# A gated mix of two attentions: two token blocks' sum moves and the value weights held behind the key-value products, and sixteen double steps with new orders of work

## The chip, the cores and the metric

The kernel runs on one core of a Trainium2 chip. The time is the device time of one execution in microseconds (us). Three executions of the kernel before took 321.81, 322.15 and 322.46 us, with a median of 322.15. One more execution was recorded by the hardware profiler; it took 322.69 us, of which the recorded span is 321.0.

The core has five engines with instruction streams of their own, which meet only at semaphores: TensorE (PE in the profile; its weight loads are shown as PEld), VectorE (DVE), ScalarE (ACT), GpSimd (POOL) and SyncE (SP), which here issues nearly all DMA transfers.

## The reference

The input x has 2048 tokens of 640 features; there are 32 heads of 20 features. Two attentions are computed from the same x and mixed by a gate per token:

```
g   = sigmoid(sum(x * gate_w))
out = g * A(x) + (1 - g) * B(x)

A: q, k, v = x @ wqkv;  pq, pk = q @ w_phi, k @ w_phi  (per head)
   phi(t) = [softmax(t), softmax(-t)]
   kv = phi(pk)^T v (head by head);  z = sum over tokens of phi(pk)
   A  = ((phi(pq) @ kv) / (phi(pq) . z + 1e-6)) @ wo

B: four segments of 512 tokens, one after the other; per head
   a_dot = causal softmax attention within the segment
   a_mem = (phi(q) @ M) / (phi(q) . z)        phi(t) = t + 1 if t > 0 else exp(t)
   o     = sigmoid(beta) * a_mem + (1 - sigmoid(beta)) * a_dot
   M, z grow by phi(k)^T v and sum of phi(k) after each segment
   B     = o @ wo
```

## The kernel before, in words

The order of instructions on every engine is written out by hand: each engine runs its instructions in the order in which the program emits them, and waits at the head of its queue until the semaphores of that instruction are there. There is no planner but the small one of the double steps (below).

**Key stage (from 10 to 56 us).** For each of 16 blocks of 128 tokens (`emit_a1`, L235 to L247) TensorE makes keys and values, ScalarE the exponentials, VectorE the sums and reciprocals, and GpSimd (VectorE for block 15) multiplies the normalised key features into `EkSn`. Right behind each block `emit_zmove` (L255) issues two transfers on SP, one for each sign. They copy 16 x 8 x 640 numbers of `EkSn` into rows of the tile `Z`, so that the sum z over all tokens can be made by adding 32 column groups of `Z` on VectorE. Block 14 fills groups 16 to 23 of part of the rows, block 15 groups 24 to 31.

**Key-value products (56 to 65 us).** `emit_kv` (L373) multiplies `EkSn` with the values, 312 small matmuls, in five accumulators `kv_ps`; `emit_kvn` (L387, VectorE) masks each into `kvn`. Between them `emit_zadd` (L263) adds column groups of `Z`: groups 1 to 8 before the last accumulator is masked, and 9 to 31 after the gate. The gate is `emit_gate` (L346, L349 on TensorE, L351 on ScalarE) and `emit_gS` (L354 to L356, three small VectorE instructions). VectorE has them in front of the remaining 46 additions.

**Weights of B.** `WvB`, `WkB`, `WqB` and the two output weights are loaded on SP after this (L437, L442). A copy of two columns on GpSimd (L435), which reads the fourth `kvn`, is written into `WvB` ahead of its load, so the load waits for that `kvn`. SP takes its instructions in order, so the four loads behind it wait as well.

**Query stage (65 to 92 us).** TensorE makes the query products `pq` (L400) in tiles of two PSUM banks, of which there are four; ScalarE makes two exponentials `Eq` of each (L407). The order is five `pq`, one value block of B (`v_ps`, L531), the transposes of the sum z (L268), four `pq`, the denominators (L470), another value block, one `pq`. The tile `Eq0` takes the memory that `EkSn` had, so the first exponential waits, among others, for the end of every transfer that reads `EkSn`. After the transposes VectorE sums z within its tile (`emit_zz`, L272 to L279), and GpSimd clears parts of `Z` (`open_stages`, L524 and L526). Ahead of that GpSimd writes the columns of ones of the value tiles `vB` (L544).

**Numerators (92 to 130 us)** use TensorE for A's numerators and for B's first projections, VectorE for scaling and GpSimd for adding the two signs (`oA`, L653), which DMA transposes turn into `oTA`.

**Double steps (130 to 310 us).** B's attention goes over 4 segments x 8 groups of 4 heads. Two groups a and b make a double step, and there are 16, numbered 0 to 15 here. A double step has five bursts: in each, TensorE makes scores in two PSUM tiles (`st_ps`, L723), ScalarE makes the exponentials of both (`PT`, L727), and GpSimd clears the upper triangle (L734). Only these two PSUM tiles exist, so each score product waits for the exponential of the tile used a burst earlier. Behind each burst comes other work of TensorE, taken from a list that one string of `PLAN` spells out:

- `h`: half a projection of 128 tokens for the next segment (five matmuls, L911, and a VectorE copy, L917); `f` and `o`: half an output row (ten or five matmuls, L855, and a VectorE copy or sum, L866 or L864).
- `B`, `C`: attention times values for the former double step's b, first three token blocks and then the last, with the memory terms and the closing of the group; `A`, `D`: the same for this step's a. The closing (`emit_epi`, L802 to L824) frees the single accumulator `nda` (L777, L785, L790).
- `x`, `y`: the rest of the feature map of k or q on VectorE (L886, L887); `z`: the DMA transpose of the q features; `t`: that of a finished row block; `u`: the last such transposes.

The matmuls have weights, and the list is cut in five parts of about equal weight, one behind each burst. The exponential of a feature map (L883, ScalarE) is no letter: it is emitted behind the first burst for one of k and q and behind the third for the other. Projection tiles have two PSUM buffers.

Of the kernel before, what the change touches and what calls it, by code (L numbers as in the profile page):

```python
# [15 lines left out]
def kernel(  # L16
# [15 lines left out]
    nc = tc.nc  # L32
    P = 128
# [3 lines left out]
    DH = 20  # L37
    KC = D // P
# [73 lines left out]
    def emit_xturn(g):  # L112
        nc.sync.dma_start_transpose(out=xq[:, g], in_=x2[512 * g:512 * g + 512, :])

    def emit_xrun(r):
        nc.scalar.copy(out=xP[:, :, r * P:(r + 1) * P].rearrange("p c (s u) -> p c s u", u=8),
                       in_=xq[:, 3].rearrange("p c (s r u) -> p c s r u", r=4, u=8)[:, :, :, r])
# [20 lines left out]
    kvn = Aw.tile([P, 2, KC, HW, DH], BF16, name="kvn")  # L138
# [90 lines left out]
    def emit_a1(sc):  # L229
        pk, pv = w2tile("pk"), w2tile("pv")  # L230
        for ps, W, n in ((pk, WkA, 320), (pv, WvA, 321)):
            by_row = [(c, bk) for c in range(KC) for bk in range(2)]
            for c, bk in by_row if sc == 0 else sorted(by_row, key=lambda t: t[1]):
                rhs = WvA[:, c, bk, :] if W is WvA else WkA[:, c, bk * 320:(bk + 1) * 320]
                nc.tensor.matmul(ps[:, bk, 0:n], lhsT=key_tokens(c, sc), rhs=rhs,  # L235
                                 start=(c == 0), stop=(c == KC - 1))
        Ek = a1w.tile([P, 2, D], BF16, name="Ek")
        for sgn in range(2):
            nc.scalar.activation(out=Ek[:, sgn, :].rearrange("p (b n) -> p b n", b=2),  # L239
                                 in_=pk[:, :, 0:320], func=ACT.Exp, scale=1.0 - 2.0 * sgn)  # L240
        nc.scalar.copy(out=vA[:, sc], in_=pv[:, :, 0:321])
        ksum = a1w.tile([P, 2 * H], F32, name="ksum")
        nc.vector.tensor_reduce(out=ksum, in_=Ek.rearrange("p s (h f) -> p (s h) f", f=DH),  # L243
                                axis=AX.X, op=ALU.add)
        krec = a1w.tile([P, 2 * H], F32, name="krec")
        nc.vector.reciprocal(out=krec, in_=ksum)  # L246
        (nc.vector if sc == NCH - 1 else nc.gpsimd).tensor_tensor(  # L247
            out=EkSn[:, sc].rearrange("p s (h f) -> p (s h) f", f=DH),
            in0=Ek.rearrange("p s (h f) -> p (s h) f", f=DH),
            in1=krec[:, :, None].to_broadcast([P, 2 * H, DH]), op=ALU.mult)  # L250

    def emit_zmove(sc):
        g, r = divmod(sc, 4)
        for sgn in range(2):
            nc.sync.dma_start(out=Z[64 * sgn + g:64 * sgn + 64:4, r:32:4] if g < 3 else  # L255
                              Z[64 * sgn + g:64 * sgn + 64:4, 8 * r:8 * r + 8],
                              in_=EkSn[:, sc, sgn, :])

    def emit_zadd(ts):
        for t in ts:  # L260
            for lo in (0, D // 2):
                cols = slice(lo, lo + D // 2)
                nc.vector.tensor_tensor(out=Z[:, 0, cols], in0=Z[:, 0, cols], in1=Z[:, t, cols], op=ALU.add)  # L263

    def emit_z(bank):
        zt_ps = bank.bitcast(BF16)[:, 0:D].rearrange("p (c t) -> p c t", c=KC)
        for j in range(KC):
            nc.tensor.transpose(out=zt_ps[:, j, :], in_=Z[:, 0, j * P:(j + 1) * P], identity=ident_b)  # L268
        return zt_ps
# [35 lines left out]
    for step in ("T0", "T1", "T2", "M0", "M1", "T3", "T4", "M2", "X0", "X1", "M3", "M4"):  # L305
        n = int(step[1])
# [4 lines left out]
        else:  # L311
# [2 lines left out]
    nc.tensor.transpose(out=gw_ps, in_=gw5, identity=ident_b[0:KC, 0:KC])  # L314
    nc.vector.tensor_copy(out=WvA[:, :, :, 320:321],
                          in_=gw_ps[:, :, None, None].to_broadcast([P, KC, 2, 1]))
    for sc in range(NCH):
        emit_a1(sc)
        emit_zmove(sc)
        if sc == 1:  # L320
            emit_xturn(3)
        if 8 <= sc < 12:
            emit_xrun(sc - 8)
        if sc == 7:
            omgh_b, CM = emit_beta()
        if sc == 5:
            nc.sync.dma_start_transpose(out=WkT, in_=A_wqkv[:, 0:D])
    x_stack.close()
    for n in range(KC):
# [3 lines left out]
    WqB = resW.tile([P, KC, D], BF16, name="WqB")  # L333
    WkB = resW.tile([P, KC, D], BF16, name="WkB")
    WvB = resW.tile([P, KC, D], BF16, name="WvB")
# [4 lines left out]
        out=xg, in0=vA[:, :, 0, 320].rearrange("p (g u) -> p u g", u=4)[:, :, :, None].to_broadcast([P, 4, 4, 4]),  # L340
# [37 lines left out]
    def emit_kv_groups(j, scs):  # L378
        for sc in scs:
            for sgn in range(2):  # L380
                for group in range(2):
                    emit_kv(j, sgn, [sc], group)

    def emit_kvn(j):
        h0, h1 = (P * j) // DH, (P * j + P - 1) // DH + 1
        g0 = TH[j][0]
        nc.vector.tensor_tensor(  # L387
            out=kvn[:, :, j, h0 - g0:h1 - g0, :],
            in0=kv_tiles[j][:, :, 0:(h1 - h0) * DH].rearrange("p s (h d) -> p s h d", d=DH),
            in1=wmw[:, j, None, h0 - g0:h1 - g0, None].to_broadcast([P, 2, h1 - h0, DH]), op=ALU.mult)  # L390
# [25 lines left out]
    for j in range(4):  # L416
        emit_kv_groups(j, range(14, NCH))
        emit_kvn(j)
    emit_zadd(range(7, 9))
    for sgn in range(2):  # L420
        emit_kv(4, sgn, [0])
# [9 lines left out]
    vBs = [resB.tile([P, 4, H, DH + 1], BF16, name=f"vB{n}") for n in range(2)]  # L431
    a3e = a3_stack.enter_context(tc.tile_pool(name="a3e", bufs=KC, side="right", reuse_waits="tile"))
    a3w = a3_stack.enter_context(tc.tile_pool(name="a3w", bufs=2, side="right", reuse_waits="tile"))

    nc.gpsimd.tensor_copy(out=WvB[:, 0, 0:2], in_=kvn[:, 0, 3, 0, 0:2])  # L435
    for W, src in ((WvB, B_wv), (WkB, B_wk), (WqB, B_wq)):
        nc.sync.dma_start(out=W, in_=src.rearrange("(c p) n -> p c n", p=P))  # L437

    WoA = WkA
# [81 lines left out]
    def open_stages():  # L521
        for n in range(2):
            for part in "kq":
                nc.gpsimd.memset(stages[part][n][:, :, DH:32], 0.0)  # L524
        for t in phiks:
            nc.gpsimd.memset(t[:, :, :, DH:32], 0.0)  # L526
# [13 lines left out]
        nc.scalar.copy(out=vBs[sc // 4][:, sc % 4, :, 0:DH].rearrange("p (b h) d -> p b h d", b=2),  # L540
                       in_=ps[:, :, 0:320].rearrange("p b (h d) -> p b h d", d=DH))

    for vB in vBs:
        nc.gpsimd.memset(vB[:, :, :, DH:DH + 1], 1.0)  # L544
    def emit_zsum():
        emit_zz(emit_z(z_den[:, 0]))
        open_stages()

    def emit_first_den():
        for n in range(NB):  # L550
# [74 lines left out]
    for ch in range(NCH):  # L625
# [4 lines left out]
        for sgn in range(2):  # L630
# [13 lines left out]
            if (ch, sgn) in EXPS:  # L644
                part = EXPS[ch, sgn]
                nc.scalar.activation(out=(phiks[1][:, 0] if part == "k" else phiq_st)[:, :, 0:DH],
                                     in_=stages[part][0][:, :, 0:DH], func=ACT.Exp)
# [10 lines left out]
        while turns_due:  # L658
            part, c = turns_due.pop(0)
# [14 lines left out]
    with ExitStack() as bctx:  # L674
# [196 lines left out]
        waiting = {"k": [], "q": []}  # L871
# [30 lines left out]
        def run_first(fns):  # L902
            if fns:
                fns.pop(0)()
# [19 lines left out]
        def half_items(s, order):  # L924
# [11 lines left out]

        PLAN = {0: ("hhhhyzoxoAoD", "hhBhyhzCooxAoD", "hhBhyhzCooxAoD", "ooBoyozCooxAoD"),
                1: ("hhBhhChhyzADtt", "hhBhxhCfhhyzAD", "hhBhxhCfhhyzADt", "hhBhxhCfhhyzAD"),  # L940
                2: ("hhBhxhChhyzADt",) + ("hhBhhCfhhyzADt",) * 3,
                3: ("fBfCffADtt", "fBftCfftAD", "fBftCfffAD", "ufBfCfffAD")}

        oT4 = oTA[:, 0:4]

# [7 lines left out]
        for dstep in range(NSEG * G // 2):  # L953
            s, gd = divmod(dstep, G // 2)
            if gd == 0 and s + 1 < NSEG:
                halves = half_items(s + 1, FIRST_SEG if s == 0 else CHUNKED)
            a, b = Step(2 * dstep), Step(2 * dstep + 1)
            items = []
            for w in PLAN[s][gd]:
                if w in "hfo":  # L960
                    items += {"h": halves, "f": fins, "o": aouts}[w].pop(0)
                elif w in "xy":
                    items.append((0.0, lambda part="kq"[w == "y"]: run_first(sums[part])))
                elif w == "z":
                    items.append((0.0, lambda: run_first(q_turns)))
                elif w == "u":
                    items += [(0.0, lambda n=n: turn_last(n)) for n in range(4)]
                elif w == "t":
                    items.append((0.0, lambda ch=turns.pop(0): emit_oT(ch)))
                else:  # L970
                    st = a if w in "AD" else prev
                    items += pv_items(st, (0, 1, 2)) if w in "AB" else pv_items(st, (3,)) + mem_items(st)
            share = sum(w for w, _ in items) / 5
            done = 0.0
            for n, burst in enumerate(bursts(a, b)):
                burst()
                if n in (0, 2):
                    run_first(waiting["kq"[n == (0 if s == 0 else 2)]])
                while items and (n == 4 or done + items[0][0] / 2 < (n + 1) * share):
                    w, fn = items.pop(0)  # L980
                    fn()
                    done += w
            prev = b
# [146 lines left out]
```

## Time and profile before

| what | us |
| --- | --- |
| median of three executions | 322.15 |
| the profiled execution | 322.69 |
| its recorded span | 321.0 |
| TensorE busy | 305.7 (95%) |
| ScalarE busy | 253.0 (79%) |
| VectorE busy | 224.3 (70%) |
| GpSimd busy | 207.7 (65%) |

TensorE's granted clock is 1.00 in every stretch. Its matmuls overlap in a pipeline, so its busy share is not a share of its peak, and a gap between two of its instructions is read from the order of time. Where a line ends in brackets, they hold the time that the engine stood idle before it, and what released it.

### The profile page before, as it was taken

The numbers are of one execution on the slowest core, as the hardware profiler recorded it, in microseconds if no ns is written. First come the engines' busy times: TensorE is split into PE (matmuls) and PEld (weight loads), VectorE is DVE, ScalarE is ACT, GpSimd is POOL, SyncE is SP. The second block draws the span as 40 slices with busy tenths as digits, with TensorE's granted clock in tenths as the row PEclk, the third lists the DMA queues.
The fourth block names the chain that finished last, engine by engine and source line by source line (L and its number), as shares of the span: only waits on it lengthen the run. The fifth ranks groups of instructions, "written<-read, shape, count | busy, mean of one in ns | idle before, by whom it ended". The sixth has DMA issues, their size and how long they took to land.

```text
span 321.0 us, 9771 instructions
## 1 busy us (share of the span) xinstructions
PE 305.7 (95%) x4024; PEld 209.8 (65%) x4024; DVE 224.3 (70%) x505; ACT 253.0 (79%) x321; POOL 207.7 (65%) x308
## 2 busy tenths in 40 slices
PE   7999999899999999899999999999999999999995
PEld 6888877754578888456556566666666666655663
DVE  3477897989779997567768577676865755454463
ACT  4677888257856548889998999999998898998953
POOL 8588599112346989856657667777777676666550
PEclk9999999999999999999999999999999999999999
DMA  7948834496007888657241363462475383222132
GB/s 226 206 111 200 207 104 130 120 310 205 1 14 124 124 125 141 135 99 85 51 68 33 67 105 71 88 101 52 80 99 121 58 117 70 68 77 51 47 88 82
DMA packets 91814, 34.22 MB, mean 107 GB/s; under 512 B 79866, under 2 KB 91770, under 8 KB 91770
## 3 DMA queue, kind: packets, MB, share of 16 engines
q1 hardware_dynamic: 91194, 32.95, 50.4%
q10 hardware_dynamic: 576, 0.66, 0.7%
q8 instruction: 31, 0.51, 0.7%
q14 instruction: 13, 0.11, 0.1%
HBM read 6.42 MB, written 2.62 MB: 28 GB/s over the span
## 4 chain that ended last, share of the span: by engine, by line
PE 62%; ACT 20%; DVE 8%; POOL 3%; DMA 3%; issue 3%; SPq 1%; ACTq 0%; DVEq 0%; POOLq 0%
ACT PT L727 17%; PE st_ps L723 8%; PE proj L855 8%; PE pk L235 7%; PE proj L531 7%; PE pv L235 6%; PE nda L777 6%; PE proj L911 5%; PE num L453 4%; PE pq L400 3%; DVE Z L263 3%; DMA x_nat<-in_A_x_dram 2%; PE kv_ps L373 2%; PE num L470 1%; DVE Eq L887 1%
## 5 line engine op out<-in xcount | busy, mean ns | idle before, releaser
L727 ACT ACTIVATE PT<-st_ps 128x1024 bf16<-128x1024 f32 x160 | 153.7, 1024 | 15.1 <-PE st_ps L723 12.5
L734 POOL TENSOR_SCALAR_AFFINE_SELECT PT<-PT 128x512 bf16<-128x512 bf16 (+1 forms) x130 | 86.1, 681 | 47.1 <-ACT PT L727 46.9
L777 PEld LDWEIGHTS <-PT 128*128 128x128 bf16 x1280 | 40.4, 96 | 8.8 <-issue 5.3
L777 PE MATMUL nda<-vB,PT 128*128 128x21 bf16 x1240 | 41.4, 173 | 0.3
L247 POOL TENSOR_TENSOR EkSn<-Ek,krec 128x1280 bf16<-128x1280 bf16 x15 | 35.1, 2360 | 9.2 <-DVE krec L246 8.5
L911 PEld LDWEIGHTS <-xTf 128*128 128x128 bf16 x300 | 26.5, 97 | 15.8 <-issue 6.7
L917 DVE CAST Z<-proj 128x320 bf16<-128x320 f32 x44 | 20.8, 487 | 22.1 <-PE proj L911 20.7
L235 PEld LDWEIGHTS <-xTf 128*128 128x128 bf16 x240 | 27.1, 113 | 5.7
L243 DVE TENSOR_REDUCE ksum<-Ek 128x64 f32<-128x1280 bf16 x16 | 23.6, 1475 | 7.7 <-ACT Ek L239 7.5
L723 PE MATMUL st_ps<-Z 32*128 32x512 bf16 (+3 forms) x256 | 25.1, 299 | 3.8 <-ACT PT L727 3.5
L501 DVE TENSOR_TENSOR tt<-num,rr 128x640 f32<-128x640 f32 x32 | 25.0, 813 | 4.5 <-POOL rr L494 1.7
L239 ACT ACTIVATE Ek<-pk 128x640 bf16<-128x640 f32 x32 | 20.8, 702 | 9.2 <-PE pk L235 8.2
L855 PE MATMUL proj<-WkA,oTA 128*128 128x320 bf16 x160 | 27.1, 300 | 1.0 <-DMA oTA<-oA 1.0
L653 POOL TENSOR_TENSOR oA<-tt 128x640 bf16<-128x640 f32 x16 | 24.6, 1545 | 5.2 <-DVE tt L501 5.0
L723 PE MATMUL st_ps<-Eq 32*128 32x512 bf16 (+3 forms) x256 | 25.0, 299 | 2.0 <-ACT PT L727 1.6
L407 ACT ACTIVATE Eq<-pq 128x1024 bf16<-128x1024 f32 x20 | 19.4, 1021 | 7.0 <-PE pq L400 5.0
L817 POOL TENSOR_TENSOR oB<-td 128x320 bf16<-128x320 f32 x22 | 19.5, 888 | 6.6 <-DVE td L814 4.7
L855 PE MATMUL proj<-WvA,oT 128*128 128x320 bf16 x120 | 22.2, 300 | 0.6 <-DVE oTA L864 0.6
L400 PE MATMUL pq<-xTf,WqA 128*128 128x512 bf16 x100 | 22.1, 379 | 0.0
L814 DVE TENSOR_TENSOR td<-nda,rec 128x640 f32<-128x640 f32 x23 | 19.0, 825 | 2.1
L531 PEld LDWEIGHTS <-xTf 128*128 128x128 bf16 x180 | 16.2, 97 | 4.6
L855 PEld LDWEIGHTS <-oTA 128*128 128x128 bf16 x160 | 13.4, 97 | 7.8 <-issue 2.7
(177 smaller groups left out, 549.9 us busy)
## 6 DMA issues: line engine op xcount, KB each, us to landing
Z<-EkSn SPq DMA_DIRECT2D x32, 160.0 KB, 2.8
out_dram<-orow SPq DMA_DIRECT2D x8, 160.0 KB, 1.8
out_dram<-oTA SPq DMA_DIRECT2D x6, 160.0 KB, 1.9
WvA<-in_A_wqkv_dram SPq DMA_DIRECT2D x2, 400.0 KB, 6.7
WvB<-in_B_wv_dram SPq DMA_DIRECT2D x1, 800.0 KB
WkB<-in_B_wk_dram SPq DMA_DIRECT2D x1, 800.0 KB, 8.0
WqB<-in_B_wq_dram SPq DMA_DIRECT2D x1, 800.0 KB, 9.7
WkA<-in_A_wo_dram SPq DMA_DIRECT2D x1, 800.0 KB, 11.4
```

The costliest lines, as they stand in the source:

```text
L235: nc.tensor.matmul(ps[:, bk, 0:n], lhsT=key_tokens(c, sc), rhs=rhs, start=(c == 0), stop=(c == KC - 1))
L247: (nc.vector if sc == NCH - 1 else nc.gpsimd).tensor_tensor(out=EkSn[:, sc].rearrange("p s (h f) -> p (s h) f", f=DH), in0=Ek.rearrange("p ...
L400: nc.tensor.matmul(pq[:, half, :], lhsT=WqA[:, c, j * P:(j + 1) * P], rhs=xq[:, 2 * qb + half, c], start=(c == 0), stop=(c == KC - 1))
L501: nc.vector.tensor_tensor(out=tt[:, sgn].rearrange("p (b h) d -> p b h d", b=2), in0=ps, in1=csb, op=ALU.mult)
L531: nc.tensor.matmul(ps, lhsT=xq[:, sc // 4, cc, sc % 4 * P:(sc % 4 + 1) * P], rhs=W[:, cc, half * 320:(half + 1) * 320], start=(cc == 0), s ...
L653: nc.gpsimd.tensor_tensor(out=oA.rearrange("p (h d) -> p h d", d=DH), in0=tt[:, 0], in1=tt[:, 1], op=ALU.add)
L723: nc.tensor.matmul(ps[:, i - i0, o:o + L - c * P], lhsT=kT[32 * i:32 * i + 32, c * P:(c + 1) * P], rhs=qT[32 * i:32 * i + 32, c * P:L], st ...
L727: nc.scalar.activation(out=PT[:, i0:i0 + 2], in_=ps, func=ACT.Exp, scale=SCALE_B)
L734: nc.gpsimd.affine_select(out=v, in_=v, pattern=[[0, n_i], [1, P]], compare_op=ALU.is_ge, fill=0.0, base=0, channel_multiplier=-1)
L777: nc.tensor.matmul(nd[:, j, i], lhsT=block(st, c)[:, i, (j - c) * P:(j - c + 1) * P], rhs=vB[:, c, 4 * st.g + i, :], start=(c == 0), stop= ...
L855: nc.tensor.matmul(ps, lhsT=oT[:, k % KC], rhs=W[:, k % KC, hs], start=(k == 0), stop=(k == n - 1))
L911: nc.tensor.matmul(ps, lhsT=xq[:, sc // 4, k, sc % 4 * P:(sc % 4 + 1) * P], rhs=W[:, k, half * 320:(half + 1) * 320], start=(k == 0), stop ...
```

## The change

There are two parts.

1. In the key stage the transfers of blocks 14 and 15 are left out of the loop. They are emitted after the fourth `kvn`: first GpSimd's copy into `WvB`, then a load of the first fifth of `WvB`, then the four held transfers, and the rest of `WvB` with the other weights behind them. The columns of ones of `vB` are written after GpSimd has cleared `Z`.
2. `PLAN` has one string for each of the 16 double steps. Two new letters `k` and `q` say where the feature exponentials stand, instead of the fixed places behind bursts one and three. One half projection moves from step 6 to step 4; `C`, `A` and `D` move ahead of some halves in steps 1, 2, 12, 14 and 15; `o` moves ahead of `A` in step 0; `y` stands ahead of the last half in steps 9 to 11.

```diff
+    HELD = (14, 15)
     for sc in range(NCH):
         emit_a1(sc)
-        emit_zmove(sc)
+        if sc not in HELD:
+            emit_zmove(sc)
...
     for j in range(4):
         emit_kv_groups(j, range(14, NCH))
         emit_kvn(j)
+
+    nc.gpsimd.tensor_copy(out=WvB[:, 0, 0:2], in_=kvn[:, 0, 3, 0, 0:2])
+    nc.sync.dma_start(out=WvB[:, 0], in_=B_wv.rearrange("(c p) n -> p c n", p=P)[:, 0])
+    for sc in HELD:
+        emit_zmove(sc)
     emit_zadd(range(7, 9))
...
-    nc.gpsimd.tensor_copy(out=WvB[:, 0, 0:2], in_=kvn[:, 0, 3, 0, 0:2])
-    for W, src in ((WvB, B_wv), (WkB, B_wk), (WqB, B_wq)):
+    nc.sync.dma_start(out=WvB[:, 1:KC], in_=B_wv.rearrange("(c p) n -> p c n", p=P)[:, 1:KC])
+    for W, src in ((WkB, B_wk), (WqB, B_wq)):
...
-    for vB in vBs:
-        nc.gpsimd.memset(vB[:, :, :, DH:DH + 1], 1.0)
     def emit_zsum():
         emit_zz(emit_z(z_den[:, 0]))
         open_stages()
+        for vB in vBs:
+            nc.gpsimd.memset(vB[:, :, :, DH:DH + 1], 1.0)
...
-        PLAN = {0: ("hhhhyzoxoAoD", "hhBhyhzCooxAoD", "hhBhyhzCooxAoD", "ooBoyozCooxAoD"),
-                1: ("hhBhhChhyzADtt", "hhBhxhCfhhyzAD", "hhBhxhCfhhyzADt", "hhBhxhCfhhyzAD"),
-                2: ("hhBhxhChhyzADt",) + ("hhBhhCfhhyzADt",) * 3,
-                3: ("fBfCffADtt", "fBftCfftAD", "fBftCfffAD", "ufBfCfffAD")}
+        PLAN = ("qhhhhyzokxooAD", "qhhBhyChkzoAoxoD", "qhhBhyChkzoAoxoD",
+                "qooBoyokzCooxAoD", "khhBhhChhqyhzADtt", "khhBhxhqChfhyzAD",
+                "khhBhxhqChfyzADt", "khhBhxhqChfhyzAD", "khhBhxhqChhyzADt",
+                "hhBhhqCfhyhzAtD", "hhBhhqCfhyhzAtD", "hhBhhqCfhyhzAtD",
+                "fBCffADftt", "fBftCfftAD", "fBftCffADf", "ufBfCfAfDf")
...
-            for w in PLAN[s][gd]:
+            for w in PLAN[dstep]:
...
+                elif w in "kq":
+                    items.append((0.0, lambda part=w: run_first(waiting[part])))
...
             burst()
-                if n in (0, 2):
-                    run_first(waiting["kq"[n == (0 if s == 0 else 2)]])
```

## The prediction

> **What bounds the kernel now.** I read the engine totals and the transfer queues first, then the chain of waits from 50 to 94 us, then the order of time of each engine there and in the double steps. Of the page:
>
> ```profile
> PE 305.7 (95%) x4024; PEld 209.8 (65%) x4024; DVE 224.3 (70%) x505; ACT 253.0 (79%) x321; POOL 207.7 (65%) x308
> q8 instruction: 31, 0.51, 0.7%
> ```
>
> TensorE is nearly always occupied, so time goes only where it loses time or hands a stretch to another engine. One such stretch is the sum z; the chain there:
>
> ```profile
> 58.27 3.42 PE kv_ps L373 x150
> 62.21 0.99 PE kv_ps L373 x33
> 63.20 1.16 issue
> 64.36 0.74 PE kv_ps L373 x28
> ...
> 65.64 1.22 DVE eg L354
> ...
> 67.34 2.92 DVE Z L263 x13
> ...
> 74.08 3.86 DVE Z L263 x16
> 77.94 0.05 issue
> 77.99 0.58 PE z_den L268 x5
> ```
>
> TensorE stops for 1.16 us inside the products, released by nothing that the profile shows. Then VectorE carries the chain, through the gate and the additions, to the transposes (`z_den`) at 77.99. The order of time there, GpSimd, VectorE and ScalarE:
>
> ```profile
> 65.58 1.23 POOL L544 MEMSET vB<- 128x128 bf16 x2 [2.04 <-PE gt_ps L349]
> 65.64 1.21 DVE L354 TENSOR_SCALAR eg<-eg 128x16 f32<-128x16 f32 x1
> 67.17 0.17 DVE L356 TENSOR_SCALAR omgS<-gS 128x16 f32<-128x16 f32 x1
> 67.65 1.94 ACT L407 ACTIVATE Eq<-pq 128x1024 bf16<-128x1024 f32 x2 [2.04 <-DVE Z L263]
> ```
>
> The same shape takes 1.21 us beside the memset and 0.17 behind it. In the double steps, ScalarE at the starts of steps 6 and 7, then TensorE and VectorE in step 14:
>
> ```profile
> 197.80 1.94 ACT L727 ACTIVATE PT<-st_ps 128x1024 bf16<-128x1024 f32 x2 [0.41 <-PE st_ps L723]
> ...
> 209.31 1.94 ACT L727 ACTIVATE PT<-st_ps 128x1024 bf16<-128x1024 f32 x2 [0.41 <-PE st_ps L723]
> ```
>
> ```profile
> 296.04 0.57 PE L855 MATMUL proj<-WvA,oT 128*128 128x320 bf16 x3 [0.63 <-DVE oTA L864]
> ```
>
> ```profile
> 294.76 0.82 DVE L814 TENSOR_TENSOR td<-nda,rec 128x640 f32<-128x640 f32 x1
> ```
>
> Step 6 lasts 11.51 us and ScalarE waits at its head for scores: TensorE sets its length. In step 14 an output half waits for a buffer whose VectorE sum stands behind the closing of C.
>
> **Part 1: the gap.** TensorE's instruction 1473 is the first behind the gap. The instruction queue moves pieces of 16,384 bytes, 256 instructions of 64, and the two boundaries before were passed at 57.15 (961) and 60.17 (1217). After the first the piece took 0.99 us, after the second 1.67, while the four transfers of blocks 14 and 15 (issued 56.96 to 59.79, the last ring done at 64.23) were running. TensorE went on at 64.36, 4.19 us after the second crossing; after the first it needed at most 3.02, and 256 products last 2.87 (60.17 to 63.04). Held back, the transfers are not there: the wait would be 3.02 - 2.87, about 0.15, against 1.32 over the usual pitch. Ends: 0 and 1.32 saved; I take 1.2, the row of the earlier crossing.
>
> [...]
>
> **The memset.** Moved behind the clears of `Z` (L524, L526) it leaves VectorE's `eg`: 1.21 - 0.17 = 1.04. It now stands in GpSimd's idle 8.71 us before `dd` (L492), needs 1.23, and its first reader, the B products, comes 20 us later: nothing.
>
> **What VectorE makes of it.** The fourth `kvn` (about 63.3) does not move. The last products end about 1.2 earlier, at 63.9, and the gate's at 64.2; but VectorE must still mask the last accumulator (to 64.2), so `eg` starts at 64.7 instead of 65.64, and with 0.17, 0.28 and 0.2 for the three steps the additions start about 65.3 (before 67.34). 46 of them at 0.2355 (10.6 us from 67.34 to 77.94) and two pauses end at 76.1; `z_den` at 76.2: 1.8 earlier. VectorE's `zz` steps have a pitch of 0.104 both beside and after GpSimd's clears, so the shift is not lost there, and TensorE shows no stall of 0.08 from 78 to 130: it carries on. TensorE had waited 0.59 there (from 77.40), and comes 1.2 earlier too, at 76.2: both arrive together. If the gap stays, TensorE still comes at 77.4, so of the memset's 1.04 only about 0.5 counts.
>
> **The held transfers.** On SP they are now behind the fourth `kvn` (63.27), GpSimd's copy (63.54) and one new load, the first fifth of `WvB` (63.57). Issues last 0.58 each: 64.0 to 65.8. They land 2.5 to 2.7 later (page: median 2.8, at most 4.4): block 14 at 67.3, block 15 at 68.9, worst 70.2. The additions reach groups 16 at 68.6 and 24 at 72.3: covered, by 1.3 and by 3.4. Behind them in SP's queue: the rest of `WvB` issues at 66.4 and lands about 71 (whole, before, 68.7), wanted at 74.4; `WkB` to 75, wanted at 90; `WqB` and the output weights later still. No cost while these covers of 3 and 15 us hold. TensorE's next piece of instructions comes in the `pq` products, which pass 256 instructions in over ten us: also covered.
>
> The first exponential of the query stage waits for the last transfer, since `Eq0` has the memory of `EkSn`: 68.7 to 68.9 instead of 67.65. Queued behind it on ScalarE are the other `Eq`, and behind these TensorE's `pq` (four buffers). The sixth `pq`, first after `z_den` at 76.2 + 0.58, needs the fourth exponential, done 7.6 us after the first starts: free up to a start of 69.2. So the wait costs nothing at 68.9, and 1.0 at 70.2. Part 1: -1.8, of which I count -1.7 (0.1 for the tail of the wait); ends -0.5 and -2.0.
>
> **Part 2.** Prices: half a projection 0.68 us (five matmuls, L531's rows), a burst's scores 0.62, A with D 1.00 (`nda`, x40), a pair of exponentials 1.95, a feature exponential 0.63 in a row with others. Five pairs and two features are 11.0 us of ScalarE, a step's floor there.
>
> - Step 6 loses a half: TensorE's 11.2 worked (measured 11.51) becomes 10.5, ScalarE's 11.0 takes over: -0.5 (ends -0.7, 0).
> - Step 4 gains it: 10.82 with ScalarE in front; TensorE's idle there covers all but 0.1 (ends 0, +0.5). Its moved `ek` changes neighbours on ScalarE, not work.
> - Steps 9 to 11: `y` ahead of the last half lets VectorE begin the closing 0.1 to 0.2 earlier; TensorE's wait of 0.09 for `nda` goes: -0.2 for three (ends -0.4, +0.3, when the half's copy, queued behind `y`, holds a projection buffer).
> - Step 14: with A ahead of the third `f` the stall of 0.63 (0.79 over the pitch) is covered by 34 matmuls: -0.4 (ends -0.8, +0.1: A then waits for `nda`, freed by `td` at 295.5).
> - Steps 1, 2: A earlier can wait 0.4 for GpSimd's triangles, under TensorE's own wait of 0.5 for ScalarE; `x` later is not wanted before the next step. Step 15: the same under a wait of 0.55. Steps 0 and 12 keep their stalls (1.19 at 136.46 in step 0 is a DMA transpose's). Together 0, ends -0.3 and +0.8.
>
> Sum -1.0, ends -1.8 and +0.6 (they do not all go one way). Both parts: -2.7. The profiled execution took 322.69, 0.54 over the median: 320.0 there, 319.5 against 322.15.
>
> **Rivals.**
> - *Only part 1 acts* (ScalarE's exponentials turn at once into the bound where TensorE is relieved; steps 6 and 14 pass their gain on to the next wait): -1.7, 320.45. For: `ACT PT L727` waits only 12.5 us over 16 steps. Against: 0.79 of step 14 is no wait for ScalarE.
> - *The gap is not instruction supply and stays*: -0.5 - 1.0, 320.65. For: an instruction piece of 1.67 us does not by itself make 4.19. Against: the gap is exactly on a boundary.
> - *Slower: the first `Eq` waits too long.* Each us past 69.2 costs one. The gain of part 1 is gone at 70.9, of both parts at 71.9; at 72.6 the time is 322.85. For: one ring of block 15's transfers was 1.7 us later than the others' end (62.50 against 64.23), and a new load runs with them. Against: the worst landing of the page, 4.4, makes 70.2.
> - *Slower: the new orders hold VectorE's copies.* If a projection buffer waits 0.3 us more in each of ten steps, +3.0 against -2.7: 322.45. It decides from 0.27 a step.
>
> **How the numbers follow.** Forecast 0.45, only part 1 0.23, gap stays 0.13, first `Eq` late 0.07 (half of it within or above the old time), new orders hold the copies 0.12. About 0.2% (0.64 us) is what a measurement of this kernel can tell from no change. Faster: the first three and some of the others, 0.83; same 0.07; slower 0.10. Range 318.2 (part 1 at -2.0, part 2 at -1.8) to 321.6 (part 1 only by its memset, part 2 at nothing).
>
> **What the profile after would show.** No issue gap over 0.3 us in `kv_ps`; `eg` at 0.17; the first of the 46 additions near 65.3; `z_den` near 76.2; the first `Eq` near 68.7 with no wait of `pq` behind it; the first burst of step 0 near 128.6 (before 130.31); step 6 at most 11.1, step 4 at most 11.0, no TensorE stall over 0.4 in step 14. I am wrong if the gap stands on the boundary as before, if `Eq` starts behind 69.2 and `pq` waits for it, or if steps 1, 2, 4 or 15 are longer than before by over 0.3 us.

## The result and the profile after

The changed kernel takes 320.55 us (median of 7 executions, 320.22 to 321.77); the kernel before takes 322.37 (7 executions). That is 1.8 us between the medians. The ratio, which is not the quotient of the medians, is 0.9954 with a 95% interval of 0.9939 to 0.9968; by it the change is faster by 1.5 us (1.0 to 2.0). 319.5 was predicted, 2.7 below; the range of 318.2 to 321.6 holds the result. The profiled execution took 320.22 with a span of 318.5, which is 2.47 less than the profiled one of before. That pair of profiles shows more than the medians; why is seen below.

The page, engine totals and instruction queue:

```profile
PE 305.9 (96%) x4021; PEld 210.5 (66%) x4024; DVE 223.7 (70%) x505; ACT 252.6 (79%) x321; POOL 208.3 (65%) x308
q8 instruction: 31, 0.51, 0.7%
```

The engines' busy times are within 0.7 us of those before, so the time went mostly out of waits. The chain of waits of the changed kernel from 50 to 94 us (start, length, what; lines from L419 on have moved by some lines against before):

```profile
58.26 3.42 PE kv_ps L375 x159
...
62.21 0.99 PE kv_ps L375 x33
63.20 0.35 issue
63.55 0.74 PE kv_ps L375 x25
...
64.83 0.18 DVE eg L356
...
65.50 3.30 DVE Z L263 x14
...
69.90 7.45 ACT Eq L409 x8
77.35 0.04 issue
77.39 0.38 PE pq L402
77.77 0.05 issue
77.82 8.36 PE pq L402 x38
```

Before, the additions carried this chain from 67.34 to 77.94 and handed over to `z_den`. Now the additions begin at 65.5, but at 69.90 the chain passes to ScalarE's first exponential, and from there to the sixth `pq` at 77.39. That is the rival of the prediction in a mild form: the first `Eq` comes late and TensorE waits for a buffer behind `z_den`. The order of time, SP and ScalarE, shows why it comes at 69.90:

```profile
63.56 0.37 SPq L423 DMA_DIRECT2D WvB<-in_B_wv_dram  x1
63.99 3.38 SPq L255 DMA_DIRECT2D Z<-EkSn  x4
67.42 0.59 SPq L441 DMA_DIRECT2D WvB<-in_B_wv_dram  x1
```

```profile
69.90 2.85 ACT L409 ACTIVATE Eq<-pq 128x1024 bf16<-128x1024 f32 x3 [5.11 <-DVE Z L263]
```

The four issues last 3.38 us where four times 0.58 had been counted; the third alone takes 1.46. So the last is issued at 66.77, 0.97 later than worked out, and the first `Eq` starts 1.0 later than worked out. In the four profiles with both blocks held directly behind the first fifth of `WvB` and all on SP (this one, `part1_alone`, `held_alone` and `half_and_last_back` below), the four issues took 2.91 to 3.96 us together, and the first `Eq` came 2.3 to 2.8 behind their end. (ScalarE's line names an addition as its releaser, the last event ahead of it; the transfers are the wait, as the chain of `held_alone` below shows.)

Both profiles by double steps, worked out from the starts of ScalarE's exponentials of the scores (every tenth one begins a step; the last number runs to TensorE's last instruction):

```
step      0     1     2     3     4     5     6     7     8     9    10    11    12    13    14    15+end
before 11.65 11.17 11.17 11.17 10.82 11.52 11.52 11.52 10.97 11.38 11.47 11.47 11.26 10.39 11.16 18.48
after  11.28 11.08 11.08 11.16 10.67 11.72 11.24 11.51 10.97 11.38 11.40 11.38 11.21 10.41 11.01 18.20
```

From step 1 on the gains sum to 1.05 us. With one `PLAN`, steps 1 to 15 agree from profile to profile within 0.04 (step 10 of the old `PLAN`, at 11.46 to 11.72, is the exception), so differences of 0.1 can be read there. Step 0 can't be read so: in the runs below it takes between 11.3 and 12.8, whatever its order.

### The profile page after: what moved, and what is told of

It reads as the page before. It is cut to its first block, busy times and chain, and to the rows that moved or that the text cites. A ratio compares the mean times of both kernels' runs of the same rounds, so it can differ in the third digit from the quotient of the medians.

```text
span 318.5 us, 9772 instructions
## 1 busy us (share of the span) xinstructions
PE 305.9 (96%) x4021; PEld 210.5 (66%) x4024; DVE 223.7 (70%) x505; ACT 252.6 (79%) x321; POOL 208.3 (65%) x308
## 4 chain that ended last, share of the span: by engine, by line
PE 70%; ACT 19%; DVE 5%; DMA 2%; issue 2%; POOL 1%; SPq 0%; ACTq 0%; DVEq 0%; POOLq 0%
ACT PT L733 13%; PE st_ps L729 10%; PE proj L861 9%; PE proj L917 7%; PE nda L783 7%; PE pk L235 7%; PE proj L537 7%; PE pv L235 6%; PE num L459 4%; PE pq L402 3%; ACT Eq L409 2%; PE kv_ps L375 2%; DVE Z L263 1%; DMA wnat_k<-in_A_wqkv_dram 1%; PE num L476 1%
## 5 line engine op out<-in xcount | busy, mean ns | idle before, releaser
L923 DVE CAST Z<-proj 128x320 bf16<-128x320 f32 x44 | 20.8, 486 | 22.3 <-PE proj L917 21.0
L861 PE MATMUL proj<-WkA,oTA 128*128 128x320 bf16 x160 | 27.8, 300 | 0.7 <-DMA oTA<-oA 0.7
L729 PE MATMUL st_ps<-Eq 32*128 32x384 bf16 (+3 forms) x256 | 25.4, 299 | 1.5 <-ACT PT L733 1.1
## 6 DMA issues: line engine op xcount, KB each, us to landing
WkA<-in_A_wo_dram SPq DMA_DIRECT2D x1, 800.0 KB, 10.1
```

Of the source, the lines that this page charges most:

```text
L729: nc.tensor.matmul(ps[:, i - i0, o:o + L - c * P], lhsT=kT[32 * i:32 * i + 32, c * P:(c + 1) * P], rhs=qT[32 * i:32 * i + 32, c * P:L], st ...
L861: nc.tensor.matmul(ps, lhsT=oT[:, k % KC], rhs=W[:, k % KC, hs], start=(k == 0), stop=(k == n - 1))
```

## The experiments

The theory after this comparison: the hold shortens the gap and frees the gate, but it makes the first `Eq` late, and part of the gain is lost there; the orders of the double steps act by themselves. Rivals: the double steps take the shift of part 1 back; or step 0 and the end are shorter only because of the shift.

**Each part alone.** Both are cut from the shown diff: `part1_alone` has the new key stage with the old `PLAN`, `part2_alone` the reverse. Each ratio below is against executions of the kernel before that were made together with it.

> The held transfers and the moved memset, with the old orders of the double steps. Theory (the first Eq starts at 69.9, 0.7 past the 69.2 that TensorE's four buffers allow, and that 0.7 is lost there): the first burst of step 0 at 129.3 as in the changed kernel, steps as before, the time 1.0 below before (ratio 0.997). Rival (the shift by part 1 is taken back in the double steps, whose waits on transposes do not move): first burst at 129.3, but steps 0 to 3 longer by 0.3 or more in sum, time within 0.6 of before.

Measured: 321.44 against 322.00, ratio 0.9976 (0.9964 to 0.9987); first burst at 129.30; steps 1 to 15 as before, but for step 10 (11.63). The places in the profile are those of the theory; of its 1.0 us the times show 0.56 between the medians and 0.8 by the ratio.

> The new orders of the double steps with the old key stage. Theory (the orders act by themselves): first burst at 130.3, steps 0, 4, 6, 14 and the tail shorter by 0.37, 0.15, 0.28, 0.15 and 0.28, step 5 longer by 0.2, together -1.4 (ratio 0.9957). Rival (step 0 and the tail are shorter only because part 1 brings everything a microsecond forward against the transposes and the weight loads): step 0 and the tail as before, together -0.7 (0.9978).

Measured: 321.04, ratio 0.9970 (0.9956 to 0.9985). Every step from 1 to the end has the length of the changed kernel within 0.02. The theory's 1.4 had 0.37 of step 0 in it, which is not this part's. The parts add up within the intervals: 0.56 and 0.96 against 1.82 between the medians, 0.8 and 1.0 against 1.5 by the ratios. Both rivals fall, except that step 0 belongs to neither part: it took 11.33 with the old order (`part1_alone`) and 11.27 with the new.

**The two edits of part 1 apart.** `held_alone` is the kernel before with the held transfers, `memset_alone` with the memset behind the clears of `Z` only:

```diff
-    for vB in vBs:
-        nc.gpsimd.memset(vB[:, :, :, DH:DH + 1], 1.0)
     def emit_zsum():
         emit_zz(emit_z(z_den[:, 0]))
         open_stages()
+        for vB in vBs:
+            nc.gpsimd.memset(vB[:, :, :, DH:DH + 1], 1.0)
```

> The held transfers alone: the memset in its old place, the old orders. Theory (the gap falls to about 0.4 to 0.6 in pitch, but the memset still holds eg, and the late first Eq at 69.9 then lies under the additions): eg 1.2 us, additions end at 77.4, z_den near 77.4, no wait of pq behind it, first burst of step 0 at 129.8, time 0.5 below before (0.9984). Rival (the hold is worth what the prediction gave it, 1.2, and the memset's share is the smaller one): first burst at 129.2, time 1.1 below before.

> The moved memset alone. Theory (TensorE itself comes to z_den at 77.4, so of the 1.04 only half counts): gap of 0.9 to 1.4 still there, eg 0.17, additions end at 77.1, z_den at 77.4, first Eq at 67.7, first burst of step 0 at 129.75, time 0.55 below before (0.9983). [...]

Measured: the hold alone 321.58, ratio 0.9985 (0.9971 to 0.9999), the memset alone 321.25, ratio 0.9969 (0.9957 to 0.9981). The memset gained more than its theory's 0.9983, which lies outside the interval. The expectation of the time of `held_alone` was met, its reason was not: `eg` took 0.17 there, too. GpSimd's line in the order of time of `held_alone`:

```profile
70.67 1.24 POOL L550 MEMSET vB<- 128x128 bf16 x2 [6.65 <-DMA Z<-EkSn]
```

The memset stands in its old place in the program, but `vB` has memory that the held transfers read, so it waits for them and is gone from the gate by itself. With the hold, moving the memset frees nothing further. Its chain of waits shows the wait for the transfers, too:

```profile
67.60 2.80 DMA Z<-EkSn
...
70.63 7.45 ACT Eq L409 x8
```

And the memset alone, without the hold, brings what part 1 brings as a whole, or more. The chain of waits of `memset_alone` from 58 to 94 us:

```profile
63.17 0.69 issue
63.85 0.74 PE kv_ps L373 x25
...
64.88 10.81 PE pq L400 x50
75.69 1.36 PE v_ps L531 x10
77.05 0.28 PE z_den L268 x5
77.33 8.63 PE pq L400 x40
```

The gap is still there, but from 64.88 on TensorE runs without a wait: neither the additions nor the first `Eq` is on the chain.

**The whole change without the hold.** `no_hold` is `memset_alone` with the new `PLAN`.

> The changed kernel without its held transfers: the moved memset and the new orders alone, SP's order as before. Theory (with the memset moved, the shorter gap that the hold gives and the later first Eq cancel): gap 0.9, first Eq at 67.2, z_den about 0.55 later than in the changed kernel against the first product but no wait of pq behind it; the time equal to the changed kernel's within 0.3, ratio to before 0.994 to 0.996. Rival (the hold is worth 1 us by itself): time 1 us above the changed kernel, ratio 0.9985.

Measured: 320.02, ratio 0.9943 (0.9926 to 0.9959). Within the intervals the hold of both blocks is worth nothing in the changed kernel; the theory holds.

**The late first `Eq`.** Three doses of it: block 15's transfers on ScalarE's queue, block 15 held alone, and the held transfers behind all of `WvB`.

Block 15's transfers on ScalarE's queue (`block15_on_scalar`):

```diff
-    for sc in HELD:
-        emit_zmove(sc)
+    emit_zmove(14)
...
     emit_gate()
+    emit_zmove(15, nc.scalar)
     emit_gS()
```

> The changed kernel, but block 15's two transfers are issued by ScalarE right behind the gate's exponential instead of by SP. Theory (the first Eq waits for the last held transfer, and this wait makes TensorE's wait behind z_den): transfers issued by 65.9 and landed by 68.5, first Eq at 68.0 to 68.6, no wait of pq behind z_den, z_den still at 76.5, the time 0.6 to 0.7 below the changed kernel (ratio to before about 0.9935). Rival (the end of the sum z alone sets the stretch, and the wait of 0.53 behind z_den only takes the place of another): Eq earlier, the numerators not; the time equal to the changed kernel's.

Measured: 321.06, ratio 0.9971 (0.9944 to 0.9997). A miss. ScalarE and SP in the order of time of this kernel:

```profile
63.44 2.59 SPq L255 DMA_DIRECT2D Z<-EkSn  x2
```

```profile
64.13 1.88 ACTq L255 DMA_DIRECT2D Z<-EkSn  x2
69.70 2.85 ACT L409 ACTIVATE Eq<-pq 128x1024 bf16<-128x1024 f32 x3 [5.45 <-DMA Z<-EkSn]
```

The second queue did not spare the slow issues, the second on SP now took 2.01 and the second on ScalarE 1.22, but side by side the four were over earlier: 10.1 us behind the first key-value product, against 10.9 in the changed kernel. The landing was not earlier: the first `Eq` starts 13.77 behind that product, against 13.43. So 0.8 us of issuing was saved, and nothing of the landing. What held the landing here is not shown. In addition the additions, which wait for this data, ended at 77.34 instead of 76.45.

Block 15 held alone (`only15_held`):

```diff
-    HELD = (14, 15)
+    HELD = (15,)
```

> The changed kernel, but block 14's transfers stand in the loop again and only block 15's are held. Theory (the load on the rings at 60 to 64 us delays the instruction piece): half of the load, gap between 0.35 and 1.16, about 0.7; first Eq at about 68.7, so no wait of pq; net within 0.4 of the changed kernel. Rival (the gap is there or not, by the last transfers of block 15 alone): gap 0.35, Eq at 68.7, time 0.6 below the changed kernel.

Measured: 319.88, ratio 0.9933 (0.9915 to 0.9951), the lowest median of the study. The gap is 0.35 as with both held, the first `Eq` at 68.59. From its chain of waits:

```profile
62.91 0.35 issue
63.27 0.74 PE kv_ps L375 x26
...
64.29 10.81 PE pq L402 x50
75.11 1.36 PE v_ps L537 x10
76.47 0.28 PE z_den L268 x5
76.74 8.63 PE pq L402 x40
```

The gap, the first `Eq` and the time are those of the rival: with block 14's transfers running the gap is as short as without. Whether block 15's are what lengthens it, this one profile can't show (see the gap below). The interval overlaps with those of the changed kernel and `no_hold`, so the three are not told apart by their times.

The held transfers behind all of `WvB` (`moves_behind_wvb`):

```diff
+    nc.sync.dma_start(out=WvB[:, 1:KC], in_=B_wv.rearrange("(c p) n -> p c n", p=P)[:, 1:KC])
     for sc in HELD:
         emit_zmove(sc)
...
-    nc.sync.dma_start(out=WvB[:, 1:KC], in_=B_wv.rearrange("(c p) n -> p c n", p=P)[:, 1:KC])
```

> The changed kernel with the four held transfers behind the whole of WvB instead of its first fifth. Theory (each us that the first Eq starts past 69.2 costs one): first Eq at 72 to 73, numerators 2 to 3 us later than in the changed kernel, time 322.6 to 323.6, slower than before. Rival (TensorE's order takes it up, or the additions wait instead): first Eq late as well, but the numerators less than 1 us later, time below before.

Measured: 323.42, ratio 1.0036 (1.0022 to 1.0051): slower than before. From its chain of waits:

```profile
64.95 6.60 DMA Z<-EkSn
...
73.14 7.45 ACT Eq L409 x8
80.59 0.04 issue
80.63 8.79 PE pq L402 x40
```

This is the rival "the first `Eq` waits too long" built on purpose, and it is priced as the prediction had it. The additions waited for the same transfers (2.63 us), so that `z_den` is late, too; the first `Eq` is the later of the two. In seven of the kernels, counted from the first key-value product (so that earlier differences drop out):

```
                     z_den   first Eq   first numerator   numerator - z_den   numerator - Eq
memset_alone         20.66      10.91        34.25              13.59              23.34
only15_held          20.11      12.40        33.71              13.60              21.31
half_and_last_back   20.38      13.23        34.03              13.65              20.80
changed kernel       20.11      13.43        34.23              14.12              20.80
part1_alone          20.24      13.87        34.67              14.43              20.80
held_alone           20.59      14.08        34.88              14.29              20.80
moves_behind_wvb     22.86      16.88        37.68              14.82              20.80
```

The numerators begin 13.60 behind `z_den` or 20.80 behind the first `Eq`, whichever is later. In the other profiles they begin 13.60 (`no_hold`, `only15_fill_step0`) or 13.73 (both of before, `part2_alone`, `count_plus64`, `block15_on_scalar`) behind `z_den`. The wait is free up to 7.20 ahead of `z_den`, and costs its full length from there on. The prediction had 7.0 (76.2 against 69.2).

**What the gap is.** `count_plus64` adds 32 small transposes ahead of the key stage to the kernel before:

```diff
-    nc.tensor.transpose(out=gw_ps, in_=gw5, identity=ident_b[0:KC, 0:KC])
+    for _ in range(33):
+        nc.tensor.transpose(out=gw_ps, in_=gw5, identity=ident_b[0:KC, 0:KC])
```

> The kernel before with 32 more small transposes of the same tile ahead of the key stage (64 more instructions of TensorE, the result unchanged). Theory (the gap stands where TensorE crosses from one piece of 256 instructions to the next): the gap comes 64 instructions earlier, at kv product number 252 or so in place of 284, about 0.75 us earlier against the products, and is as long or longer (1.3 to 2.1), since the piece arrives no sooner. Rival (the gap belongs to that accumulator or to a wait of those products): it stays at number 284. The time says nothing here; the transposes cost 2 to 5 us at the start.

Measured: 322.47 (one execution). The chain of waits of that kernel:

```profile
62.16 0.22 PE kv_ps L374
62.38 0.53 issue
62.91 1.46 PE kv_ps L374 x61
```

The stop is now ahead of product 252, exactly 32 products earlier, and there is none at product 284. It goes with the count of instructions, not with an accumulator. The transposes' 2 to 5 us do not show: this line begins at 62.16, that of the kernel before at 62.21. The theory's 1.3 to 2.1 did not come either: the stop was 0.75 from product to product, against 1.36. So `before_again` runs the kernel before once more:

> The kernel before once more, for a second profile. Theory (the gap of 1.36 in the first profile was a long one; the three kernels with the old order of transfers showed pitches of 0.75 to 0.89 at the boundary): a gap of 0.7 to 0.9 at product 284, and the time about 0.4 below that of the first profile. Rival (1.36 belongs to this kernel): 1.3 to 1.4 again.

Measured: 323.02 (one execution; not 0.4 lower but 0.33 higher, with a long step 0 that the last section shows), and from its chain of waits:

```profile
62.88 0.68 issue
63.56 0.74 PE kv_ps L373 x28
```

From product to product this is 0.88, as in `memset_alone` (0.89), `part2_alone` (0.89) and `no_hold` (0.88). The 1.36 on which the prediction rests was a long one. With block 15 held it is 0.55 to 0.61 in five profiles, 0.82 in two, and 0.89 with the transfers behind `WvB`. Up to the gap this last kernel issues the same instructions as the changed one. TensorE behind the gap, then two windows ahead of it in `moves_behind_wvb` (length, busy time of five engines with counts, PEclk, DMA share, GB/s):

```profile
63.80 0.74 PE L375 MATMUL kv_ps<-vA,EkSn 128*64 128x80 bf16 x29 [0.69 <-issue]
```

```profile
60.00:62.00 2.00, 2.00 (x104) 1.91 (x98) 1.40 (x7) 0.00 (x0) 0.00 (x0) 1.00 0.04 8
62.00:63.80 1.80, 1.01 (x34) 0.80 (x33) 1.80 (x7) 0.00 (x0) 0.21 (x1) 1.00 0.00 0
```

With a DMA share of 0.04 and 0.00 the stop is as long as the usual one of before. So the transfers are not needed for it: that they lengthen it is likely from the five shorter ones, but not shown. From one boundary to the next (product 156 to product 284, 256 instructions) the changed kernel took 3.37 us without transfers, and this one 3.72; the prediction had at most 3.02. In four profiles (`part2_alone`, `held_alone`, `no_hold`, `memset_alone`) TensorE stopped ahead of product 156, too, one boundary earlier, for 0.2 to 0.9 us.

**The double steps.** `half_and_last_back` is the changed kernel with three strings of `PLAN` changed (steps 4, 6 and 15):

```diff
-  "khhBhhChhqyhzADtt" ... "khhBhxhqChfyzADt" ... "ufBfCfAfDf"
+  "khhBhhChhqyzADtt"  ... "khhBhxhqChfhyzADt" ... "ufBfCfffAD"
```

> The changed kernel with the half projection back in step 6 and the old order in step 15. Read by the steps. Theory (the half is the cause of the changes of steps 4 to 6, and A between the output halves that of the last step): step 6 back to 11.5 from 11.24, step 5 back to 11.5 from 11.72, step 4 at 10.8; step 15 with the tail back to 18.48 from 18.20. Rival (the feature exponentials' new places are the cause): steps 4 and 5 stay at 10.67 and 11.72, only step 6 changes; the tail stays at 18.2, its gain coming from step 14.

Measured: 319.90 (one execution); steps 4 to 6 took 10.25, 11.78 and 11.51 us, together 33.54; the changed kernel 33.63, the kernel before 33.86. The half costs step 4 0.42 and gives step 6 only 0.27. So the 0.23 gained in these three steps comes from the other edits of their strings, which bring 0.32, and the moved half takes 0.09 of that back. For step 4 both the theory and the rival missed; for step 5 and the end the rival was near. Step 4's string here is the old one with `k` and `q` put in, so the new places of the feature exponentials give that step 0.57; step 5, with `k` and `q` in new places and one `f` and `h` exchanged, is 0.26 longer than before. Step 15 with the end took 18.27: its order is worth 0.07 of the 0.28; the other 0.21 comes with the steps before it, of which 12 and 14 were changed.

**Step 0.** In every profile but that of the kernel below TensorE stands for 0.7 to 1.4 us in step 0 until the last DMA transpose of A's rows has come. `only15_fill_step0` is `only15_held` with a half projection of step 1 put ahead of the output halves, and an output half given back:

```diff
-  "qhhhhyzokxooAD", "qhhBhyChkzoAoxoD"
+  "qhhhhyzkxhooAD", "qhBhyChkzooAoxoD"
```

> Only block 15 held, and in step 0 a half projection of the next segment stands where an output half waits for the last transpose of A's rows; step 1 has that output half instead. Theory (TensorE's stall of 1.26 in step 0 is a wait for that transpose, and 0.68 of other work covers as much of it): the stall falls to 0.6, steps 0 and 1 together 0.4 to 0.6 shorter, the time about 319.4, ratio 0.992. Rival (SP's other transposes or ScalarE set the end of step 0): steps 0 and 1 together the same as with block 15 alone (22.73), time 319.9.

Measured: 321.76, ratio 1.0002 (0.9980 to 1.0024): the gain of `only15_held` is gone. Steps 0 and 1 took 12.26 and 11.62, together 1.15 more than with block 15 alone. TensorE and then VectorE in step 0:

```profile
137.78 0.84 PE L861 MATMUL proj<-WkA,oTA 128*128 128x320 bf16 x5 [2.11 <-DVE Z L923]
```

```profile
135.23 0.76 DVE L892 TENSOR_SCALAR Z<-Z 128x640 bf16<-128x640 bf16 x1
136.02 1.13 DVE L893 SCALAR_TENSOR_TENSOR Z<-Z 128x640 bf16<-128x640 bf16 x1
137.24 0.49 DVE L923 CAST Z<-proj 128x320 bf16<-128x320 f32 x1
```

The wait for the transpose is gone, and in its place the output half waits 2.11 us for a projection buffer: the new half's copy (L923) stands in VectorE's queue behind the feature map of k, which has to read the old stage first. This is the prediction's last rival, held copies, in one step.

## Why the prediction was right, and where its steps were not

The sign and the range held, and the memset's effect on `eg` (1.21 to 0.17); 1.8 came instead of 2.7, two thirds of it (1.5 by the ratio). The held transfers brought nothing, and that the double steps came to their sum is luck. By its steps:

- *The gap, 1.2.* That the stop belongs to the instruction count was right, the term was mis-sized. It was taken from the one gap shown, 1.36, and from one earlier crossing. The usual pitch there is 0.88, and with the hold 0.55 to 0.61 in five profiles of eight: 0.33 at best. That the crossing needs at most 3.02 us without the transfers was wrong: 3.37 in the changed kernel. Between the profiled pair the gap differs by 0.8, and 0.5 of that is the one long stop. That the transfers lengthen the stop was not shown, and `moves_behind_wvb` has the usual 0.89 without them.
- *The memset, 1.04.* `eg` went from 1.21 to 0.17 as worked out. Of that, 0.58 reached the numerators in `memset_alone`, counted from the first product against `before_again` (34.25 and 34.83), near the 0.5 that the prediction gave it if the gap stays. Why `eg` takes longer beside the memset is not shown. That the memset costs nothing in its new place held: 1.23 us at 81.16, in GpSimd's idle time. That the hold moves it away anyway was not seen.
- *The held transfers, "costs nothing".* This failed. The threshold was right (69.2), the landing was not: 68.9 was worked out from issues of 0.58, and the third took 1.46. The trace of before had such an issue among the same transfers, 1.57 for block 14's second at 57.53; the prediction took 0.58 for all. The numerators begin 0.52 later than `z_den` allows (14.12 against 13.60). The worst case of 70.2 was the nearer one.
- *The sum of part 1, -1.7.* 1.02 between the two profiles at the first burst; 0.56 between medians. The gap's 0.33 at best and the late `Eq`'s 0.52 leave nothing for the hold, and `no_hold` shows the same in the time; the gain is that the memset has left the gate.
- *Part 2, -1.0.* 1.05 from step 1 on, 0.96 as a kernel of its own. The sum was right with terms that were not, which is luck. Step 6 gained 0.28 for 0.5 (the half itself is worth 0.27 there, not its 0.68 of work); step 4, which was to lose 0.1, gained 0.15 (0.57 by the new places of the feature exponentials, counted as no work and so as nothing, less 0.42 for the half), and step 5 lost 0.20, where nothing was said. Steps 9 to 11 gained 0.16 for 0.2, steps 1 and 2 0.18 and the end 0.28 for nothing.
- *Step 14, -0.4.* It gained 0.15. The end named with it (A then waits for the accumulator) came in its place, in the changed kernel's order of time:

```profile
293.67 0.60 PE L783 MATMUL nda<-vB,PT 128*128 128x21 bf16 x18 [0.22 <-DVE td L820]
```

- *The rivals.* "Only part 1 acts" (320.45) and "the gap stays" (320.65) are nearer to the measured 320.55 than the forecast, but out as they were told: part 2 brought its sum, and the gap goes with the count of instructions, as `count_plus64` shows (ahead of product 252 in place of 284), though no view names what TensorE waits for there. In its price the second was nearly right, since the gap's 1.2 hardly came. "Slower by the first `Eq`" was real, with a start of 69.90 where 71.9 would have been the point of no gain; `moves_behind_wvb` reached 73.14 and is slower.
- *The signs named beforehand.* `eg` at 0.17, step 4 at 10.67 and no stall over 0.4 in step 14 came; the additions at 65.4 (65.3) and `z_den` at 76.6 (76.2) are near. A gap over 0.3 remained (0.35), step 6 took 11.24 (at most 11.1), and the first burst came at 129.3 (128.6). One sign of being wrong came true: the first `Eq` started behind 69.2 and `pq` waited for it.

What stays open: why one transfer of a close group issues so slowly (it came on SP's queue, 2.01, and on ScalarE's, 1.22, and nothing here separates that further); why the gap is 0.55 in some executions with block 15 held and 0.82 or 0.89 in others, and what the transfers add to it; and which of the steps 12 and 14 gives the end its 0.21.

## What to carry to other kernels

When a transfer is moved later, find what reuses the memory that it reads, not only who reads what it writes: here the first exponential and a memset had waits on it, one costing all that the move gained (0.52 us against 0.33 at best) and one doing another edit's work. A stall seen in one profile is one sample (1.36 here, and 0.88 in the next profile of the same kernel); its size belongs in a sum only after a look at a second execution, or as the low end. Filling an engine's wait with work pays only if the queue behind that work (here VectorE's copy that frees the buffer) has room at that moment; without it steps 0 and 1 took 1.15 us more.

## What the runs showed of the hardware

**The granted clock was once halved behind a short stall.** In `before_again` step 0 took 12.82 instead of 11.65. The windows of three microseconds, with the same columns:

```profile
132.00:135.00 3.00, 2.37 (x19) 0.98 (x17) 1.32 (x3) 3.00 (x4) 2.52 (x4) 1.00 0.68 136
135.00:138.00 3.00, 2.19 (x10) 0.84 (x10) 1.85 (x5) 1.24 (x2) 1.76 (x2) 0.62 0.87 162
138.00:141.00 3.00, 3.00 (x44) 1.89 (x41) 1.41 (x3) 2.68 (x3) 0.63 (x1) 0.81 0.62 118
```

The clock is at one half (0.50 from 136 to 138) for 3.41 us, from 135.72 to 139.14, across the end of the stall for the transpose, and six matmuls of an output half take 1.78 us instead of 0.99. The other profiles with this stall, of 0.70 to 1.35 us, show no halved clock there, so the stall alone does not decide it. The idle time was 1.19 us at this place, and TensorE was busy for 2.06 of the 3.41 us ahead of the halved clock. What halves it is not shown. In `only15_fill_step0`, with a stall of 2.11, five of twelve executions had a mean clock of 0.987 to 0.989 and took 322.99 to 323.43, and the other seven 0.995 to 1.00 and 321.00 to 321.77, a difference of 1.8 us between the means. The profiled execution is one of the seven and shows no halved clock at its stall, so where the five lost theirs is not shown. Step 0 of `before_again` was 1.17 us longer than in the first profile of the same kernel, whose stall was 1.02 with the clock at 1.00.

**One issue of a close group can take several times the usual.** Most transfers of 160 KB issued in 0.53 to 0.62 us. In most groups of four in close succession one took 0.77 to 2.07 (1.05 and 1.58 in the first profile of before, 1.54 and 1.46 in the changed kernel), and two did in the group on SP and ScalarE together; of a pair, too, one can be slow (1.54 and 2.01 in `only15_held`). In the two groups of four of `count_plus64` none took over 0.60. What decides it is not shown.
